# A sparse-attention and MoE kernel whose threshold pick among nine numbers on VectorE is replaced by eight pads that GpSimd writes behind the masked scores

## The chip, the cores and the metric

The kernel runs on one core of one Trainium2 chip. The metric is the device time of one execution in microseconds (us). Before the change it was 1723.53 us, the median of three runs (1721.57 to 1724.83). A core has five engines that work side by side, each in the order of its own instruction list: TensorE (PE in the profile, its weight loads are PEld), VectorE (DVE), ScalarE (ACT), GpSimd (POOL) and SyncE (SP), which here issues the transfers. An instruction that needs another engine's result waits for a semaphore, and everything behind it on its own engine waits with it.

## The reference

An attention in which every query keeps only its 32 largest scores, followed by a two-layer network with a squared ReLU:

```
scores = scale * q @ k.T                      # 8 batches, 8 heads, 576 x 576, 64 wide
kth    = the 32nd largest score of each row
scores = where(scores >= kth, scores, -1e9)
attn   = exp(scores - max) / (sum + 1e-9)
x      = attn @ v                             # heads side by side: 4608 tokens x 512
h      = x @ w_in                             # 512 x 2048
g      = s * relu(h)**2 + b
out    = g @ w_out                            # 2048 x 512
```

q, k and v are float32, the two weight matrices come in float64. Products are made of high and low halves of float32 numbers, so that they keep float32's precision.

## The kernel before, in words

**Tiles.** The scores of 128 queries against 576 keys are one tile; 288 tiles make up the attention (9 for each pair of heads, 4 pairs in a batch, 8 batches). A loop over steps (L813) keeps several tiles under way: in step i the scores of tile i + 2 are multiplied, the candidates of tile i are searched, tile i - 1 gets its cut, and tile i - 2 its threshold, its mask and its transposes. The hidden chunks of the network run between them, about one a step once a batch of attention is done, paced by `pace` (L804).

**The threshold of a tile.** VectorE takes the 8 largest of each of 8 groups of 72 scores (`groups`, L270), and from these 64 candidates, in three rounds (`chain`, L277 to L286), the 24th largest. GpSimd (`cut_at`) takes the upper 16 bits of that candidate less a half as the cut (L293), makes the bias of the exponential (L294), and clears the lower 16 bits of the candidate in place (L295). ScalarE (`side`, L301) writes `wt`: 1 for a score below the cut and -1 for the others, and adds these up into `cnt`. With n scores at or above the cut, `cnt` is 576 - 2n. GpSimd (`window`, L306) multiplies `wt` by the scores, so that those at or above the cut become negative. VectorE (`wmax`, L313) takes the 8 largest of `wt`: these are the places n + 1 to n + 8 of the row. `pick` (L318) then compares `cnt` with nine constants in `sel` and so picks the 32nd place among nine numbers, the cut candidate itself and these eight. `mask` (L323) sets the exponentials `e` to zero where the score is below that threshold `th`, and sums the rest. TensorE transposes the result (`put`, L352), ScalarE takes its high halves `ph` (L357), VectorE the low halves `pl` (L363), and TensorE multiplies with v (`attend`, L391, L392).

**What sets the order.** No scheduler moves these parts. Every step emits its parts by one of three written lists, ORDER_FIRST while weights are converted, ORDER_MAIN in most steps, ORDER_LAST from shortly before the last batch, and each engine keeps the order in which its parts were emitted. `wt`, `e`, the score bank `s_ps` and the transpose bank `tp` have one buffer each: the next transposes wait until `pl` has read the bank. At the end a row whose threshold could not be proven sets a flag, and then a second, plain and much longer path computes the whole problem again.

Of the kernel before, what the change touches and what calls it, by code (L numbers as in the profile page):

```python
# [18 lines left out]
P = 128  # L19
# [3 lines left out]
CHUNKS = [(0, 0), (1, P), (2, 2 * P + D), (3, 3 * P + D)]  # columns of each 128 queries; the last 64 sit between  # L23
# [16 lines left out]
# weight steps before the first tile  # L40
WPRE = 2
# hidden chunks before the end of a block at which the next is split, after the attention
SPL = 4
# weight pieces under way in a step
WPS = 2
ENGINES = {getattr(mybir.EngineType, e) for e in ("PE", "Activation", "DVE", "Pool", "SP")}
# the order in which a step emits the parts of the tiles under way: while the weights are
# converted, in most steps, and from shortly before the last batch
ORDER_FIRST = """
    g fetch gs sc wmax cut store av c0 sq o prep exp add sums wb xs prepo hi scale side pick  # L50
# [3 lines left out]
    g sc exp wb cut add gs wmax av prep scale prepo c0 pick wa c1 xs h gA split mask hi lows wc  # L54
# [3 lines left out]
    wb gs add sc exp wmax wa av g cut hi c0 prep wc pick c1 relu prepo h o scale split c2 mask  # L58
# [7 lines left out]
def fast_path(ctx, tc, q, k, v, w_in, w_out, s_in, b_in, out, flag):  # L66
# [48 lines left out]
    # the weights come in float64, as its bits; a step makes float32 parts of 256 columns  # L115
# [20 lines left out]
    def weight_step(n):  # L136
# [14 lines left out]
        # a float64 exponent (a zero's too) that float32 has not is farther than 221 here  # L151
# [53 lines left out]
    def prep(j, x, hl, c0, c1, rest):  # L205
        """PE transposes of k's or q's rows; returns the emitter of what reads them."""
# [65 lines left out]
    def chain(t, k):  # L272
        """Three rounds of 8 maxima; the first two leave out the lower candidates of the groups."""
        low = t.cand.rearrange("p (g n) -> p g n", n=8)[:, :, : (3, 3, 5, 5, 8)[k]]
        if k == 0:
            t.wl = sb.tile([P, 24], F32, name="wl", tag="wl", bufs=3)
# [11 lines left out]
    def cut_at(t):  # L288
        """The 24th candidate's upper 16 bits less a half, and the maximum for exp."""
# [5 lines left out]
        nc.gpsimd.memset(cut16[:, 30:31], 0)  # L295

    def side(t):
        """1 for the scores below the cut, -1 for the others, and their sum."""
        t.wt = sb.tile([P, S], F32, name="wt", tag="wt", bufs=BUFS["wt"])
        t.cnt = sb.tile([P, 2], F32, name="cnt", tag="cnt", bufs=3)  # L300
        nc.scalar.activation(  # L301
            t.wt, t.sc.bitcast(I16)[:, 1::2], AF.Sign, bias=t.half, scale=-1.0, accum_out=t.cnt[:, 0:1]
        )

    def window(t):
        nc.gpsimd.tensor_tensor(out=t.wt, in0=t.sc, in1=t.wt, op=ALU.mult)  # L306
# [808 lines left out]
```

## Time and profile before

| What | Value |
|---|---|
| Time, median of three runs | 1723.53 us |
| Lowest and highest run | 1721.57 and 1724.83 us |
| Span of the profiled execution, first to last instruction | 1721.7 us |
| PE busy | 1563.8 us, 91% |
| DVE busy | 1460.6 us, 85% |
| ACT busy | 1321.5 us, 77% |
| POOL busy | 1247.8 us, 72% |

The profile gives the span of the profiled execution and no separate figure for what lies around it; the span is 1.8 us below the median of the three runs. Shares of busy time are means over stages of unlike kind: in the first 215 us the weights are converted beside the first attention tiles, until about 301 us there is hardly any network to compute, then attention and network run together until 1376 us, and the end is mostly network. A line in the profile is named by the kernel's line, its engine, its operation, and the buffers written and read (out<-in, buffer numbers left out).

### The profile page before, as it was taken

The page shows a single profiled execution, that of the slowest core. Times are in us where ns is not written, and L with a number is a line of the kernel's source. Part 1 is how long each engine was busy: PE and PEld are TensorE (multiplying, and loading weights), DVE is VectorE, ACT ScalarE, POOL GpSimd, SP SyncE. Part 2 cuts the span into 40 slices and gives each one's busy share as a digit, 9 for nine tenths or more (in the row PEclk, how much of TensorE's full clock was granted, in tenths as well). Part 3 has the DMA queues.
Part 4 walks back from the last instruction along what each step waited for, and adds up shares of the span by engine and source line. Part 5 has one row for each costly group of instructions (what it writes and reads, how often), then busy time and mean ns, then how long its engine had stood idle before and what let it go on. Part 6 is the DMA issues. An engine that isn't in the chain of part 4 may idle for free.

```text
span 1721.7 us, 36778 instructions
## 1 busy us (share of the span) xinstructions
PE 1563.8 (91%) x10001; PEld 1352.9 (79%) x10001; DVE 1460.6 (85%) x6631; ACT 1321.5 (77%) x3042; POOL 1247.8 (72%) x2240
## 2 busy tenths in 40 slices
PE   4778878998999999999999999999999999999997
PEld 3445546877888887878798888898888879898886
DVE  6999977999999999999999989998998987786500
ACT  5777766888888888888888888888887887776532
POOL 6777746777877877777777777877777777767543
PEclk9778887999999999999999999999999999999999
DMA  4433311121221212121212121211222243332110
GB/s 126 115 103 116 94 48 49 39 66 45 53 61 37 67 41 67 39 67 45 70 41 58 45 66 37 76 40 50 57 58 64 59 111 97 92 95 78 47 28 15
DMA packets 113208, 110.25 MB, mean 64 GB/s; under 512 B 47456, under 2 KB 83296, under 8 KB 112992
## 3 DMA queue, kind: packets, MB, share of 16 engines
q1 hardware_dynamic: 112992, 107.81, 23.4%
q8 instruction: 82, 1.34, 0.3%
q14 instruction: 134, 1.10, 0.2%
HBM read 65.01 MB, written 23.86 MB: 52 GB/s over the span
## 4 chain that ended last, share of the span: by engine, by line
PE 49%; DVE 31%; ACT 7%; POOL 6%; issue 5%; DMA 1%; SPq 1%; ACTq 0%; POOLq 0%; DVEq 0%
PE h L493 16%; PE ops L517 14%; DVE e L323 6%; DVE cand L270 5%; PE s_ps L255 5%; PE tp L352 5%; DVE wl L313 3%; DVE pl L363 3%; DVE jk L318 2%; POOL wt L306 2%; PE av L391 2%; PE av L392 2%; DVE rt L142 2%; ACT wt L301 2%; PE s_ps L201 1%
## 5 line engine op out<-in xcount | busy, mean ns | idle before, releaser
L306 POOL TENSOR_TENSOR wt<-sc,wt 128x576 f32<-128x576 f32 x288 | 426.8, 1482 | 215.5 <-ACT wt L301 212.3
L493 PE MATMUL h<-x,wih 128*128 128x256 f32 x2176 | 433.6, 294 | 7.5 <-POOL x L485 4.3
L270 DVE MAX8 cand<-sc 128x8 f32<-128x72 f32 x2304 | 400.9, 218 | 4.0 <-ACT sc L264 4.0
L493 PEld LDWEIGHTS h<-x,wih 128*128 128x128 f32 x2176 | 341.4, 190 | 25.6 <-POOL x L485 16.9
L493 PE MATMUL h<-x,wil 128*128 128x256 f32 x1088 | 307.7, 283 | 0.0
L310 ACT ACTIVATE e<-sc,nb 128x576 f32<-128x576 f32 x288 | 223.0, 774 | 91.7 <-PE tq L353 69.4
L323 DVE SCALAR_TENSOR_TENSOR e<-sc,tall,e 128x576 f32<-128x576 f32 x288 | 279.8, 972 | 10.5 <-ACT e L310 9.5
L313 DVE MAX8 wl<-wt 128x8 f32<-128x576 f32 x288 | 215.5, 748 | 51.4 <-POOL wt L306 50.9
L301 ACT ACTIVATE wt<-sc,nb 128x576 f32<-128x576 int16 x288 | 223.3, 775 | 18.5 <-POOL nb L293 16.4
L352 PE MATMUL tp<-idr,e 128*128 128x128 f32 x1152 | 187.0, 287 | 54.3 <-DVE pl L363 37.8
L508 POOL TENSOR_TENSOR gl<-rt,gh 128x256 fp32r<-128x256 f32 x288 | 213.1, 740 | 28.8 <-PE ops L517 4.6
L264 ACT ACTIVATE sc<-s_ps 128x576 f32<-128x576 f32 x288 | 185.4, 644 | 63.3 <-DVE e L323 32.3
L517 PE MATMUL ops<-woh,gl 128*128 128x512 f32 x576 | 229.2, 398 | 0.9 <-POOL gl L508 0.5
L517 PE MATMUL ops<-woh,gh 128*128 128x512 f32 x576 | 227.4, 395 | 1.0 <-POOL gh L507 1.0
L517 PE MATMUL ops<-wol,gh 128*128 128x512 f32 x576 | 227.9, 396 | 0.0
L352 PEld LDWEIGHTS tp<-idr,e 128*128 128x128 f32 x1152 | 143.0, 147 | 100.6 <-DVE pl L363 54.5
L363 DVE TENSOR_TENSOR pl<-tp,ph 128x512 fp32r<-128x512 f32 x252 | 172.8, 686 | 51.9 <-ACT ph L357 50.4
L493 PEld LDWEIGHTS h<-x,wil 128*128 128x128 f32 x1088 | 207.5, 191 | 0.0
L507 POOL TENSOR_SCALAR gh<-rt 128x256 fp32r<-128x256 f32 x288 | 129.9, 451 | 94.6 <-ACT rt L502 81.4
L499 ACT ACTIVATE rt<-h 128x256 f32<-128x256 f32 x288 | 109.1, 379 | 102.1 <-PE h L493 100.6
L357 ACT ACTIVATE ph<-tp 128x512 fp32r<-128x512 f32 (+1 forms) x288 | 169.2, 587 | 16.9 <-PE av L391 12.5
L255 PE MATMUL s_ps<-ka,qs 128*128 128x288 f32 x512 | 158.0, 323 | 19.5 <-ACT qm L221 9.2
(107 smaller groups left out, 3692.3 us busy)
## 6 DMA issues: line engine op xcount, KB each, us to landing
kb<-ka SPq DMA_DIRECT2D x128, 144.0 KB, 2.5
out_dram<-osb SPq DMA_DIRECT2D x72, 128.0 KB, 2.4
raw<-in_k_dram SPq DMA_DIRECT2D x64, 128.0 KB, 2.3
x<-in_moe_w_in_dram SPq DMA_DIRECT2D x32, 256.0 KB, 3.1
x<-in_moe_w_out_dram SPq DMA_DIRECT2D x32, 256.0 KB, 2.9
xd<-avu SPq DMA_DIRECT2D x28, 288.0 KB, 2.2
raw<-in_q_dram SPq DMA_DIRECT2D x56, 128.0 KB, 2.2
raw<-in_v_dram SPq DMA_DIRECT2D x56, 128.0 KB, 2.2
```

Source lines behind the costliest of these rows:

```text
L255: nc.tensor.matmul(flat[:, hf * 288 : (hf + 1) * 288], st, kx[:, hf * 288 : (hf + 1) * 288], start=(m == 0), stop=(m == last),)
L270: nc.vector.max(t.cand[:, g * 8 : g * 8 + 8], t.sc[:, g * GW : (g + 1) * GW])
L301: nc.scalar.activation(t.wt, t.sc.bitcast(I16)[:, 1::2], AF.Sign, bias=t.half, scale=-1.0, accum_out=t.cnt[:, 0:1])
L306: nc.gpsimd.tensor_tensor(out=t.wt, in0=t.sc, in1=t.wt, op=ALU.mult)
L310: nc.scalar.activation(t.e, t.sc, AF.Exp, bias=t.nb, scale=scale)
L313: nc.vector.max(t.wl[:, 16:24], t.wt)
L323: nc.vector.scalar_tensor_tensor(t.e, t.sc, t.th, t.e, op0=ALU.is_ge, op1=ALU.mult, accum_out=t.pair.ssum[:, t.i : t.i + 1])
L352: nc.tensor.transpose(tp[:, c, :], t.e[:, c * P : (c + 1) * P], idf)
L363: nc.vector.tensor_tensor(out=pl[:, :, dst], in0=tp, in1=ph[:, :, dst].bitcast(F32), op=ALU.subtract)
L493: nc.tensor.matmul(h, wi[a][:, cc, fs], k.x[cc][:, c, :], start=(n == 0), stop=(n == last))
L508: nc.gpsimd.tensor_tensor(out=gl, in0=rt, in1=gh.bitcast(F32), op=ALU.subtract)
L517: nc.tensor.matmul(k.ops[t], g[:, ts_], wo[w][:, fc, :], start=(fc == 0 and i == 0), stop=(fc == NFC - 1 and i == 2),)
```

## The change

`pick` and its constants go. Instead GpSimd writes eight more numbers, `pads`, behind the 576 of `wt`, and the maximum over 584 columns finds the threshold as its eighth value. Pad j is (2j - 527 + cnt) * -1e30. With n scores at or above the cut, n - 24 of the eight pads are large and positive and the others large and negative, so the eighth largest of the 584 is the 32nd place of the row when n is between 24 and 31. The clearing of the candidate's lower bits (L295) goes too. The maxima, the threshold and the row's sum now stand in one buffer `chk`, nine numbers for each tile, in place of `ssum`, `tall` and the last third of `wl`.

```diff
-    sel = const.tile([P, NG + 1], F32, name="sel")
-    for j in range(NG + 1):
-        nc.gpsimd.memset(sel[:, j : j + 1], float(S - 2 * (TOPK - j)))
+    pads = const.tile([P, PADS], F32, name="pads")
+    for j in range(PADS):
+        nc.gpsimd.memset(pads[:, j : j + 1], float(2 * j - (S - 2 * 24 - 1)))
...
-            t.wl = sb.tile([P, 24], F32, name="wl", tag="wl", bufs=3)
+            t.wl = sb.tile([P, 16], F32, name="wl", tag="wl", bufs=3)
...
-        nc.gpsimd.memset(cut16[:, 30:31], 0)
...
-        t.wt = sb.tile([P, S], F32, name="wt", tag="wt", bufs=BUFS["wt"])
+        t.wt = sb.tile([P, S + PADS], F32, name="wt", tag="wt", bufs=BUFS["wt"])
...
-        nc.gpsimd.tensor_tensor(out=t.wt, in0=t.sc, in1=t.wt, op=ALU.mult)
+        nc.gpsimd.tensor_tensor(out=t.wt[:, :S], in0=t.sc, in1=t.wt[:, :S], op=ALU.mult)
+        nc.gpsimd.tensor_scalar(t.wt[:, S:], pads, t.cnt[:, 0:1], -PADK, op0=ALU.add, op1=ALU.mult)
...
-        nc.vector.max(t.wl[:, 16:24], t.wt)
-
-    def pick(t):
-        jk = sb.tile([P, NG + 1], F32, name="jk", tag="jk", bufs=1)
-        t.th = t.pair.tall[:, t.i : t.i + 1]
+        nc.vector.max(t.pair.chk[:, t.i, 0:8], t.wt)
+
+    def mask(t):
+        chk = t.pair.chk[:, t.i]
         nc.vector.scalar_tensor_tensor(
-            jk, sel, t.cnt[:, 0:1], t.wl[:, 15:24], op0=ALU.is_equal, op1=ALU.mult, accum_out=t.th
+            t.e, t.sc, chk[:, 7:8], t.e, op0=ALU.is_ge, op1=ALU.mult, accum_out=chk[:, 8:9]
         )
 
-    def mask(t):
-        nc.vector.scalar_tensor_tensor(
-            t.e, t.sc, t.th, t.e, op0=ALU.is_ge, op1=ALU.mult, accum_out=t.pair.ssum[:, t.i : t.i + 1]
-        )
...
-        nc.vector.tensor_reduce(tmin[:, 0, pr.i : pr.i + 1], pr.tall[:, :n], axis=AX.X, op=ALU.min)
+        nc.vector.tensor_reduce(tmin[:, 0, pr.i : pr.i + 1], pr.chk[:, :n, 7:9], axis=AX.XY, op=ALU.min)
...
-        nc.vector.tensor_scalar(pr.ri[:, :n], pr.ssum[:, :n], 1e-9, None, op0=ALU.add)
+        nc.vector.tensor_scalar(pr.ri[:, :n], pr.chk[:, :n, 8], 1e-9, None, op0=ALU.add)
...
-            elif op == "pick":
-                bk and pick(bk)
```

In the three lists of the order the word `pick` goes, and nothing else in them changes. VectorE's list of a step of ORDER_MAIN before, from the last round of the candidates of one tile (`wl<-cand`) over the maximum of `wt` and the pick of the tile two before it to its mask and low halves:

```order
L286 MAX wl<-cand 128x8
L270 MAX cand<-sc 128x8 x5
L313 MAX wl<-wt 128x8
L277 MAX wl<-cand 128x8
L318 SCALAR_TENSOR_TENSOR jk,tall<-sel,cnt,wl 128x9
L279 MATCH_REPLACE cand<-wl,cand 128x8x3
L270 MAX cand<-sc 128x8
L323 SCALAR_TENSOR_TENSOR e,ssum<-sc,tall,e 128x576
L363 TENSOR_TENSOR pl<-tp,ph 128x4x128
```

The same stretch of VectorE's list in the changed kernel:

```order
L289 MAX wl<-cand 128x8
L273 MAX cand<-sc 128x8 x5
L318 MAX chk<-wt 128x8
L280 MAX wl<-cand 128x8
L282 MATCH_REPLACE cand<-wl,cand 128x8x3
L273 MAX cand<-sc 128x8
L322 SCALAR_TENSOR_TENSOR e,chk<-sc,chk,e 128x576
L362 TENSOR_TENSOR pl<-tp,ph 128x4x128
```

The pick has gone from between the two first rounds of the candidates, and nothing stands in another place. GpSimd's list of such a step before, from one product `wt` over the network's halves (`gh`, `gl`) and the cut (`nb`) to the next `wt`:

```order
L306 TENSOR_TENSOR wt<-sc,wt 128x576
L507 TENSOR_SCALAR gh<-rt 128x256
L508 TENSOR_TENSOR gl<-rt,gh 128x256
L293 TENSOR_SCALAR nb<-wl 128x1
L294 TENSOR_SCALAR nb<-wl 128x1
L295 MEMSET wl 128x1
L187 TENSOR_TENSOR hl<-raw,hl 128x5x64
L306 TENSOR_TENSOR wt<-sc,wt 128x576
```

And in the changed kernel:

```order
L309 TENSOR_TENSOR wt<-sc,wt 128x576
L310 TENSOR_SCALAR wt<-pads,cnt 128x8
L507 TENSOR_SCALAR gh<-rt 128x256
L508 TENSOR_TENSOR gl<-rt,gh 128x256
L296 TENSOR_SCALAR nb<-wl 128x1
L297 TENSOR_SCALAR nb<-wl 128x1
L190 TENSOR_TENSOR hl<-raw,hl 128x5x64
L309 TENSOR_TENSOR wt<-sc,wt 128x576
L310 TENSOR_SCALAR wt<-pads,cnt 128x8
```

The pads stand right behind the product, ahead of the network's halves, and the clearing has gone from behind the two cuts. The lists of TensorE, ScalarE and SyncE are as they were.

## Rows read from the trace of the kernel before

**Rows 1.** The page's first part: the span, and the busy time of each engine with its share of the span and its instructions.

```profile
span 1721.7 us, 36778 instructions
PE 1563.8 (91%) x10001; PEld 1352.9 (79%) x10001; DVE 1460.6 (85%) x6631; ACT 1321.5 (77%) x3042; POOL 1247.8 (72%) x2240
```

**Rows 2.** Busy time by stage: start and end of the stretch, its length, then for each engine its busy us and (x) its instructions, the granted TensorE clock as a share of full speed, the DMA engines' share, and GB/s.

```profile
43.00:215.00 172.00, 134.45 (x548) 89.78 (x549) 168.92 (x699) 129.01 (x292) 127.56 (x225) 0.79 0.37 107
215.00:301.00 86.00, 65.81 (x314) 48.18 (x313) 66.05 (x330) 57.62 (x126) 46.68 (x86) 0.78 0.18 48
301.00:430.00 129.00, 116.19 (x787) 103.36 (x786) 123.10 (x563) 106.53 (x246) 96.34 (x172) 0.99 0.19 50
430.00:860.00 430.00, 401.35 (x2723) 354.41 (x2724) 405.92 (x1896) 363.12 (x838) 335.73 (x591) 1.00 0.21 55
860.00:1376.00 516.00, 497.54 (x3414) 447.90 (x3412) 477.13 (x2190) 431.17 (x999) 399.60 (x718) 1.00 0.21 54
1376.00:1677.00 301.00, 293.07 (x1940) 263.81 (x1939) 187.58 (x835) 199.96 (x468) 202.23 (x370) 0.99 0.28 79
```

**Rows 3.** What TensorE's matmuls waited for longest in the stretches from 301 to 430, 430 to 860 and 860 to 1376 us, one row for each: us in total, times, the longest.

```profile
PE tp L352 <- DVE pl L363: 7.9, 6, 2.3
...
PE tp L352 <- DVE pl L363: 17.6, 21, 1.1
...
PE tp L352 <- DVE pl L363: 9.0, 11, 1.1
```

**Rows 4.** The costliest groups of instructions by line, shapes kept apart: busy us, mean ns of one | idle us of the engine just before them, and what ended it.

```profile
L270 DVE MAX8 cand<-sc 128x8 f32<-128x72 f32 x2304 | 400.9, 218 | 4.0 <-ACT sc L264 4.0
L323 DVE SCALAR_TENSOR_TENSOR e<-sc,tall,e 128x576 f32<-128x576 f32 x288 | 279.8, 972 | 10.5 <-ACT e L310 9.5 <-ACT ka L213 0.2
L313 DVE MAX8 wl<-wt 128x8 f32<-128x576 f32 x288 | 215.5, 748 | 51.4 <-POOL wt L306 50.9
L318 DVE SCALAR_TENSOR_TENSOR jk<-sel,cnt,wl 128x9 f32<-128x9 f32 x288 | 106.2, 369 | 7.0 <-ACT e L310 0.7 <-DVE wl L277 0.7 <-ACT sc L264 0.4
...
L507 POOL TENSOR_SCALAR gh<-rt 128x256 fp32r<-128x256 f32 x288 | 129.9, 451 | 94.6 <-ACT rt L502 81.4 <-PE tp L352 10.3 <-PE ops L517 0.2
L294 POOL TENSOR_SCALAR nb<-wl 128x1 f32<-128x1 f32 x288 | 59.7, 207 | 0.0
L295 POOL MEMSET wl<- 128x1 int16 x288 | 29.3, 102 | 0.0
L426 POOL TENSOR_SCALAR avl<-ri 128x128 f32<-128x128 f32 x16 | 6.3, 411 | 0.3
```

**Rows 5.** The pick's own line: minimum, median and maximum of its duration in ns, first and last start.

```profile
L318 DVE SCALAR_TENSOR_TENSOR jk<-sel,cnt,wl x288: 211/231/1289, 30.5 to 1620.1; 128x9 f32<-128x9 f32 x144
```

**Rows 6.** The timeline of VectorE through one step (start us, us, instruction, and in brackets the idle time before it and what ended it).

```profile
912.08 0.75 DVE L313 MAX8 wl<-wt 128x8 f32<-128x576 f32 x1
912.74 0.17 DVE L277 MAX8 wl<-cand 128x8 f32<-128x24 f32 x1
912.93 0.23 DVE L318 SCALAR_TENSOR_TENSOR jk<-sel,cnt,wl 128x9 f32<-128x9 f32 x1
913.09 0.08 DVE L318 DVE_READ_ACCUMULATOR jk<-sel,cnt,wl 128x1 f32 x1
913.09 0.09 DVE L279 MATCH_VALUE_LOAD cand<-wl,cand 128x8 f32 x1
913.16 0.17 DVE L279 MATCH_REPLACE8 cand<-wl,cand 128x24 f32<-128x24 f32 x1
913.25 0.22 DVE L270 MAX8 cand<-sc 128x8 f32<-128x72 f32 x1
913.39 1.40 DVE L323 SCALAR_TENSOR_TENSOR e<-sc,tall,e 128x576 f32<-128x576 f32 x1
```

**Rows 7.** The timeline of GpSimd beside it (the two cuts and the low halves of k's or q's rows), and then of VectorE and GpSimd five us later, around another pick.

```profile
912.93 0.20 POOL L293 TENSOR_SCALAR nb<-wl 128x1 f32<-128x1 int16 x1
913.08 0.20 POOL L294 TENSOR_SCALAR nb<-wl 128x1 f32<-128x1 f32 x1
913.30 0.88 POOL L187 TENSOR_TENSOR hl<-raw,hl 128x320 fp32r<-128x320 f32 x1
...
917.92 1.25 DVE L318 SCALAR_TENSOR_TENSOR jk<-sel,cnt,wl 128x9 f32<-128x9 f32 x1
919.11 0.08 DVE L279 MATCH_VALUE_LOAD cand<-wl,cand 128x8 f32 x1
...
917.74 1.41 POOL L421 TENSOR_TENSOR avu<-avu,avl 128x576 f32<-128x576 f32 x1
```

**Rows 8.** The first and the last of 131 tiles (1 until 215 us, 10 until 301, 11 until 430, 34 until 860, 48 until 1376, 27 after) whose maximum on VectorE starts less than 0.2 us behind the end of their `wt` on GpSimd: the product and the maximum, in the timeline.

```profile
85.45 1.93 POOL L306 TENSOR_TENSOR wt<-sc,wt 128x576 f32<-128x576 f32 x1 [2.27 <-ACT wt L301]
87.42 0.76 DVE L313 MAX8 wl<-wt 128x8 f32<-128x576 f32 x1 [0.61 <-POOL wt L306]
...
1617.75 1.42 POOL L306 TENSOR_TENSOR wt<-sc,wt 128x576 f32<-128x576 f32 x1
1619.20 0.76 DVE L313 MAX8 wl<-wt 128x8 f32<-128x576 f32 x1 [1.93 <-POOL wt L306]
```

**Rows 9.** The pick's line by stage: start and end of the stretch, its length, VectorE's busy us in it with (x) the instructions, two for each pick, the granted clock, the DMA share and GB/s.

```profile
43.00:215.00 172.00, 8.38 (x53) 0.79 0.37 107
215.00:301.00 86.00, 5.94 (x32) 0.78 0.18 48
301.00:430.00 129.00, 10.54 (x50) 0.99 0.19 50
430.00:860.00 430.00, 30.92 (x168) 1.00 0.21 55
860.00:1376.00 516.00, 38.78 (x196) 1.00 0.21 54
1376.00:1677.00 301.00, 13.17 (x74) 0.99 0.28 79
```

**Rows 10.** What VectorE waited for longest over the whole span, after the output's wait at the end: us in total, times, the longest.

```profile
DVE wl L313 <- POOL wt L306: 50.9, 69, 5.4
DVE pl L363 <- ACT ph L357: 50.4, 63, 3.8
```

More of the change, by code (lines that the diff above doesn't have):

```diff
@@ L28 @@
 PW = 384
+PADS = 8
+PADK = 1.0e30
 NEG = -3.0e38
@@ L49 @@
 ORDER_FIRST = """
-    g fetch gs sc wmax cut store av c0 sq o prep exp add sums wb xs prepo hi scale side pick
+    g fetch gs sc wmax cut store av c0 sq o prep exp add sums wb xs prepo hi scale side
     split wc qk c1 lo gA c2 win relu h mask resth gC lows c3 second avout restl gB c4 put wa load
@@ L53 @@
 ORDER_MAIN = """
-    g sc exp wb cut add gs wmax av prep scale prepo c0 pick wa c1 xs h gA split mask hi lows wc
+    g sc exp wb cut add gs wmax av prep scale prepo c0  wa c1 xs h gA split mask hi lows wc
     qk resth lo side load o store relu second fetch restl c2 win gB c3 gC c4 avout sq put sums
@@ L57 @@
 ORDER_LAST = """
-    wb gs add sc exp wmax wa av g cut hi c0 prep wc pick c1 relu prepo h o scale split c2 mask
+    wb gs add sc exp wmax wa av g cut hi c0 prep wc  c1 relu prepo h o scale split c2 mask
     resth lo restl c3 qk lows xs sums gA side load win avout gC put sq gB fetch c4 second store
@@ L294, in cut_at @@
         nc.gpsimd.tensor_scalar(t.nb, t.wl[:, 0:1], -scale, 0.0, op0=ALU.mult, op1=ALU.add)
-        nc.gpsimd.memset(cut16[:, 30:31], 0)
     def side(t):
-        t.wt = sb.tile([P, S], F32, name="wt", tag="wt", bufs=BUFS["wt"])
+        t.wt = sb.tile([P, S + PADS], F32, name="wt", tag="wt", bufs=BUFS["wt"])
         t.cnt = sb.tile([P, 2], F32, name="cnt", tag="cnt", bufs=3)
         nc.scalar.activation(
-            t.wt, t.sc.bitcast(I16)[:, 1::2], AF.Sign, bias=t.half, scale=-1.0, accum_out=t.cnt[:, 0:1]
+            t.wt[:, :S], t.sc.bitcast(I16)[:, 1::2], AF.Sign, bias=t.half, scale=-1.0, accum_out=t.cnt[:, 0:1]
         )
     def window(t):
-        nc.gpsimd.tensor_tensor(out=t.wt, in0=t.sc, in1=t.wt, op=ALU.mult)
+        nc.gpsimd.tensor_tensor(out=t.wt[:, :S], in0=t.sc, in1=t.wt[:, :S], op=ALU.mult)
+        nc.gpsimd.tensor_scalar(t.wt[:, S:], pads, t.cnt[:, 0:1], -PADK, op0=ALU.add, op1=ALU.mult)
     def expo(t):
@@ L634, in fast_path @@
         pr.qs, pr.ks, pr.vs, pr.avs, pr.hl, pr.raw = [None] * 2, [None] * 2, [None] * 2, None, {}, {}
-        pr.ssum = pr.tall = None
+        pr.chk = None
         pr.cols = sorted(order)
@@ L819, in fast_path @@
         bk = tiles[i - 2] if 2 <= i <= NT + 1 else None
-        if cur is not None and cur.pair.ssum is None:
+        if cur is not None and cur.pair.chk is None:
             pr = cur.pair
-            pr.ssum = sb.tile([P, NC9], F32, name="ssum", tag="ssum", bufs=2)
-            pr.tall = sb.tile([P, NC9], F32, name="tall", tag="tall", bufs=2)
+            pr.chk = sb.tile([P, NC9, 9], F32, name="chk", tag="chk", bufs=2)
             pr.nb = sb.tile([P, 2, NC9], F32, name="nb", tag="nb", bufs=2)
```

## The prediction

> **What bounds the kernel now.** I read the busy shares first, then the busy times by stage, then what TensorE waits for, and last the lines of VectorE. Over the whole span TensorE is busy for 91% and VectorE for 85% [rows 1], which by itself makes TensorE the bound. By stage it looks different [rows 2]. From 43 to 215 us VectorE is busy for 168.92 of 172 us, 98%, and TensorE for 78%: there VectorE is the bound. From 301 to 430 us VectorE has 95% and TensorE 90%; from 430 to 860 us 94% and 93%; from 860 to 1376 us 92% and 96%; from 1376 us on TensorE has 97% and VectorE 62%. So both engines are nearly full through the middle, and what VectorE gives back is worth something only where TensorE stands idle for it: 12.8, 28.7 and 18.5 us of idle TensorE in the three middle stages (length less busy time), of which 7.9, 17.6 and 9.0 us are waits of the transposes `tp` until VectorE has made the low halves `pl` of the tile before [rows 3]. That is the place at which the change can pay after 301 us; ahead of 215 us all that VectorE saves should count.
>
> **What goes.** 288 picks of 369 ns on average, 106.2 us of VectorE's busy time [rows 4]. That is not what they cost the engine. In a plain step the pick starts at 912.93 and the next instruction at 913.09 [rows 6]: 0.16 us of the queue, since the 231 ns of its median [rows 5] reach into the next instruction. The mean is 138 ns above the median, 39.7 us over 288 tiles, and the longest pick takes 1289 ns. One of these shows why: it begins at 917.92 and ends at 919.17, while GpSimd works from 917.74 to 919.15 on a sum with two inputs [rows 7]. The pick has two tensor inputs in SBUF as well, and it ends with the other engine's instruction. I call this a hold.
>
> The Trainium skill (GPSIMD Engine Reference, section Specifications) says that GpSimd's SBUF interfaces are shared with VectorE, with contention for VectorE instructions that have two SBUF inputs. The trace agrees here (1289 ns against 231). Taken strictly the rule speaks against the change: the hold belongs to the meeting of the two engines and not to the pick, and the mask, which also has two SBUF inputs, would meet the same GpSimd instruction. That is the first rival below.
>
> How much of the hold goes: without the pick the mask would be reached 0.30 us after the place where the pick stood (913.09 to 913.39, [rows 6]), so up to 0.3 us of a hold is covered by work with one input and the rest goes over to the mask. The long one would give back 0.3 of 1.0 us, a hold under 0.3 us all of it. Bounds 0 and 0.14 us for each tile; most holds must be short, since half of the picks have none and the mean is 0.14, so I take 0.09. With the 0.16 that makes 0.25 us for each tile.
>
> **What comes.** The maximum reads 584 columns instead of 576: from 218 ns at 72 to 748 ns at 576 columns [rows 4] it is 1.05 ns a column, so 8 ns. VectorE keeps 0.24 us for each tile.
>
> GpSimd's pads, 128x8 with one tensor input: nearest rows are 207 ns for one column and 411 ns for 128 columns; from 207 at 1 to 451 at 256 columns it is 0.96 ns a column [rows 4], which makes 0.21 us. No row has a number per partition as the operand of GpSimd's instruction, so the bounds are 0.15 us (from one cut to the next, 912.93 to 913.08, [rows 7]) and 0.41 us; I take 0.2. The clearing that goes (102 ns, [rows 4]) stands elsewhere, ahead of a stretch in which GpSimd mostly waits for ScalarE, and I cost it at nothing: between 0 and 0.1 us a tile gained. GpSimd is busy for 72%, so its total is no matter. What matters is the place: the pads stand between `wt` and the maximum that waits for it. Behind the waiting maximum stand the first rounds of the candidates, the mask, and `pl`, for which the transposes wait. In 131 tiles the maximum starts less than 0.2 us behind the end of `wt`: 1 until 215 us, 10, 11, 34, 48 in the stages after that, and 27 at the end [rows 8]; the view of waits counts 69 and 50.9 us [rows 10]. There 0.2 us are added. Behind `wt` the network's halves `gh` and `gl` come 0.2 us later as well; they have slack in a step, and I cost that at nothing, up to 0.05 us a tile.
>
> The wait of the pick for `cnt` goes with it; it hid nothing (idle of 7.0 us in all, [rows 4]). The constants at the start are eight stores for nine: nothing. ScalarE, SyncE and TensorE issue the same lists.
>
> **The sum,** with half of the instruction counts in [rows 9] as tiles:
> - 43 to 215 us: 26 tiles x 0.24 = 6.2 us, VectorE is the bound and the pads lie in slack. Gain 6.
> - 215 to 301 us: 16 x 0.24 = 3.8, less 10 x 0.2 = 2.0 for pads. VectorE is idle for a quarter there. Gain 1.
> - 301 to 430 us: 25 x 0.24 = 6.0, less 11 x 0.2 = 2.2, is 3.8; the transposes wait for 7.9. Gain 3.
> - 430 to 860 us: 84 x 0.24 = 20.2, less 34 x 0.2 = 6.8, is 13.4; the transposes wait for 17.6, so it could all count. But what is late next is `ph` of ScalarE, for which `pl` waits 50.4 us over the span [rows 10], and an earlier VectorE only waits longer there. I take 60%: gain 8.
> - 860 to 1376 us: 98 x 0.24 = 23.5, less 48 x 0.2 = 9.6, is 13.9; the transposes wait for only 9.0, and TensorE is at 96%. I take half of the 9.0: gain 4.5.
> - From 1376 us on TensorE is 97% busy and VectorE waits for others; the pads lie in its idle time: 0.
>
> Together 22.5 us off the span of 1721.7, so 1699.2; the median of the runs was 1.8 us above the span, which makes 1701 us.
>
> **Rivals.**
>
> (1) The holds go over to the mask entire. VectorE then saves 0.15 us a tile: 3.9 us until 215 us, nothing until 301, 25 x 0.15 - 2.2 = 1.6 until 430, 84 x 0.15 - 6.8 = 5.8 until 860, of which 60% is 3.5, and 98 x 0.15 - 9.6 = 5.1 until 1376, of which a third is 1.7. Gain 10, time 1714. For it: the long hold in [rows 7], and a mask of 1.40 us beside the low halves `hl` [rows 6, 7]. Against it: an earlier mask can also come ahead of such an instruction, and then gains.
>
> (2) TensorE's waits for `pl` vanish altogether: 7.9 + 17.6 + 9.0 with 6 and 1.5 from the start, 42 us, time 1681. For it: the order is fixed, so a lead that VectorE wins in one step is kept until something else takes it, and earlier masks may miss GpSimd's long products. Against it: `ph` as above, and the other two thirds of a tile's path, which do not change.
>
> (3) Slower. The pads take 0.41 us rather than 0.2, with the holds passed on. A tile whose maximum waits for `wt` then loses 0.41 - 0.15 = 0.26 us: 82 such tiles from 430 to 1376 us lose 21, of which 60% reaches TensorE, 13; 21 tiles from 215 to 430 us lose 5; the start gains 4; the end loses about 1 of its 27 x 0.26. Time 1738. It decides from the point at which pads and semaphore take longer than the 0.24 us that the pick gives back. For it: half the maxima in the busy middle start at once behind `wt` [rows 8], and nothing in the trace shows this form on GpSimd. Against it: all its short instructions with one input lie between 0.10 and 0.21 us.
>
> (4) No change: what VectorE wins is spent waiting for `ph` and for the pads. 1721 to 1727 us. For it: TensorE at 96% in the longest stage. Against it: the stage at 98% of VectorE, which is certain to gain something.
>
> That the change doesn't do what it says: a row with 32 scores at or above the cut gets a threshold that nothing reaches, its sum is 0, and the plain path runs as well, many times the time. Worked out from the reference's inputs the count lies between 24 and 30 in all 36,864 rows, so I give it less than 1 in 100.
>
> **How the numbers follow.** Forecast 0.40, (1) 0.20, (2) 0.19, (3) 0.12, (4) 0.09. A change within 0.2% (3.4 us) is about what a measurement of this kernel can tell from none. Faster by more than that: the first three and little less, 0.78; within it 0.10; slower 0.12. The range goes from 1678, just under (2), to 1727, the upper end of (4); (3) and a gain above 45 us are left out.
>
> **What would show it.** Right: no line of the pick; the maximum at 756 ns; pads near 0.21 us, and VectorE's waits for them more than 50.9 us, most of the added time from 215 us on; the mean of the mask not above 972 + 50 ns [rows 4] (at 1110, 138 more, the first rival holds); TensorE's waits for `pl` in 430 to 860 us down from 17.6 to about 10; stage 43 to 215 us shorter by 6 us at the same work. Wrong: pads over 0.3 us, waits for `pl` as long as before, or a stage in the middle that becomes shorter by more than its waits for `pl`.

## The result, and the profile after

The changed kernel takes 1736.36 us (median of 4 runs, 1735.99 to 1737.29) against 1723.45 us before (median of 4, 1721.57 to 1724.83). The ratio is 1.0079, 95% interval 1.0065 to 1.0093: 12.9 us slower. The profiled execution took 1735.99 us, 1.8 us above its span.

The page's first part and its chain of waits (answers to [rows 1]; the chain gives the share of the span by engine, and the last line is that of the kernel before):

```profile
span 1734.2 us, 35701 instructions
PE 1567.4 (90%) x10001; PEld 1356.7 (78%) x10001; DVE 1399.3 (81%) x6055; ACT 1323.9 (76%) x3042; POOL 1375.0 (79%) x2239
...
PE 31%; DVE 24%; POOL 21%; ACT 12%; issue 8%; DMA 2%; SPq 1%; POOLq 0%; ACTq 0%; DVEq 0%
...
PE 49%; DVE 31%; ACT 7%; POOL 6%; issue 5%; DMA 1%; SPq 1%; ACTq 0%; POOLq 0%; DVEq 0%
```

VectorE has 61.3 us less to do and GpSimd 127.2 us more. In the chain of the kernel before, GpSimd had 6% and TensorE 49%; now GpSimd has 21% and TensorE 31%. An engine that was nearly absent from the path to the end now carries a fifth of it.

Busy time by stage, with the columns of [rows 2]:

```profile
43.00:215.00 172.00, 135.72 (x551) 90.54 (x552) 169.57 (x647) 129.83 (x293) 145.94 (x226) 0.80 0.36 107
...
430.00:860.00 430.00, 400.48 (x2709) 353.03 (x2708) 382.61 (x1714) 362.22 (x834) 369.01 (x589) 1.00 0.21 55
860.00:1376.00 516.00, 490.08 (x3348) 439.88 (x3347) 447.72 (x1966) 424.12 (x980) 441.08 (x705) 1.00 0.20 53
```

From 43 to 215 us VectorE runs 52 instructions fewer and is as busy as before (169.57 against 168.92). From 430 to 860 us it is freed by 23 us, and TensorE's idle time does not move (29.5 us against 28.7). From 860 to 1376 us TensorE's idle time grows from 18.5 to 25.9 us, while GpSimd goes from 399.60 to 441.08 of 516 us. By the timeline of the maxima, tile 156 (counted from 0) is reached at 878.3 us in both kernels, and the last tile at 1619.2 before and 1630.9 after: nothing is won or lost on balance until 878 us, and the loss falls behind it.

Three of the long waits of VectorE and ScalarE over the span (us, times, the longest), and last the second of them in the kernel before:

```profile
DVE chk L318 <- POOL wt L310: 127.1, 169, 4.0
...
ACT wt L303 <- POOL nb L296: 65.3, 83, 2.0
...
DVE pl L362 <- ACT ph L356: 51.8, 63, 4.1
...
ACT wt L301 <- POOL nb L293: 16.4, 28, 1.2
```

The maximum's wait went from 50.9 us in 69 places [rows 10] to 127.1 in 169. The second line is the one that I had no term for: ScalarE's signs, which need GpSimd's `nb`, waited 16.4 us before and wait 65.3 now.

TensorE's waits, first from 430 to 860 us, then (matmuls, and the weight load under `PEld`) from 860 to 1376 us:

```profile
PE tp L351 <- DVE pl L362: 4.8, 9, 0.8
...
PE s_ps L204 <- ACT sc L267: 10.5, 17, 1.0
...
PE tp L351 <- DVE pl L362: 0.8, 2, 0.5
...
PEld s_ps L204 <- POOL wt L310: 15.1, 18, 1.2
```

The waits for `pl` that were to go [rows 3] did go, 17.6 to 4.8 and 9.0 to 0.8 us. Others took their place: TensorE's transposes into `s_ps` (q's and k's halves, L204) now wait until ScalarE has copied the scores out of it (10.5 us, 1.1 before), and their weight loads for GpSimd (15.1 us, 4.1 before). The profile names the pads in that last line; the loads read `idr` and `hl` and not the pads, so what released them is not shown.

The groups by line that answer to [rows 4] (busy us, mean ns | idle before), then GpSimd's product after and before, and the `nb` of the kernel before:

```profile
L322 DVE SCALAR_TENSOR_TENSOR e<-sc,chk,e 128x576 f32<-128x576 f32 x288 | 273.1, 948 | 7.5 <-ACT e L314 5.7
L318 DVE MAX8 chk<-wt 128x8 f32<-128x584 f32 x288 | 219.9, 764 | 127.3 <-POOL wt L310 127.1
...
L296 POOL TENSOR_SCALAR nb<-wl 128x1 f32<-128x1 int16 x288 | 114.7, 398 | 6.3 <-DVE wl L289 3.1
...
L310 POOL TENSOR_SCALAR wt<-pads,cnt 128x8 f32<-128x8 f32 x288 | 91.9, 319 | 24.1
...
L309 POOL TENSOR_TENSOR wt<-sc,wt 128x576 f32<-128x576 f32 x288 | 427.4, 1484 | 148.8 <-ACT wt L303 145.8
...
L306 POOL TENSOR_TENSOR wt<-sc,wt 128x576 f32<-128x576 f32 x288 | 426.8, 1482 | 215.5 <-ACT wt L301 212.3
...
L293 POOL TENSOR_SCALAR nb<-wl 128x1 f32<-128x1 int16 x288 | 58.4, 203 | 18.5 <-DVE wl L286 18.4
```

The pads cost 319 ns on average. `nb`, an instruction on one number per row that nobody edited, went from 203 to 398 ns. GpSimd's and then VectorE's timeline through one step show why:

```profile
911.40 1.43 POOL L309 TENSOR_TENSOR wt<-sc,wt 128x576 f32<-128x576 f32 x1 [1.31 <-ACT wt L303]
912.92 0.27 POOL L310 TENSOR_SCALAR wt<-pads,cnt 128x8 f32<-128x8 f32 x1
913.26 0.41 POOL L507 TENSOR_SCALAR gh<-rt 128x256 fp32r<-128x256 f32 x1
913.75 0.74 POOL L508 TENSOR_TENSOR gl<-rt,gh 128x256 fp32r<-128x256 f32 x1
914.46 0.80 POOL L296 TENSOR_SCALAR nb<-wl 128x1 f32<-128x1 int16 x1
```

```profile
913.22 0.77 DVE L318 MAX8 chk<-wt 128x8 f32<-128x584 f32 x1
913.91 0.17 DVE L280 MAX8 wl<-cand 128x8 f32<-128x24 f32 x1
914.11 0.09 DVE L282 MATCH_VALUE_LOAD cand<-wl,cand 128x8 f32 x1
...
914.41 0.80 DVE L322 SCALAR_TENSOR_TENSOR e<-sc,chk,e 128x576 f32<-128x576 f32 x1
```

The product ends at 912.83, the pads begin at 912.92 and end at 913.19, the maximum begins at 913.22: the pads put 0.36 us between product and maximum, not 0.2. Behind them on GpSimd's queue stand `gh`, `gl` and only then `nb`, which starts at 914.46, just behind the mask's start at 914.41. It stands until the mask ends at 915.21, 0.80 us for a 0.2 us instruction.

The hold of [rows 7] thus works in both directions. The Trainium skill (SBUF — State Buffer, section "Who interferes with whom") says that the ports which VectorE and GpSimd share are an exclusive lock, that a VectorE instruction with two SBUF inputs contends with a GpSimd instruction that reads SBUF, and that the order of issue decides which of the two blocks. This trace agrees (`nb`, issued 0.05 us behind the mask, took 0.80 us against a median of 192 ns).

### The profile page after: what moved, and what is told of

It is laid out like the page before. It is cut to its first block, busy times and chain, and to the rows that moved or that the text cites. A ratio compares the mean times of both kernels' runs of the same rounds, so it can differ in the third digit from the quotient of the medians.

```text
span 1734.2 us, 35701 instructions
## 1 busy us (share of the span) xinstructions
PE 1567.4 (90%) x10001; PEld 1356.7 (78%) x10001; DVE 1399.3 (81%) x6055; ACT 1323.9 (76%) x3042; POOL 1375.0 (79%) x2239
## 4 chain that ended last, share of the span: by engine, by line
PE 31%; DVE 24%; POOL 21%; ACT 12%; issue 8%; DMA 2%; SPq 1%; POOLq 0%; ACTq 0%; DVEq 0%
PE h L493 10%; PE ops L517 9%; POOL wt L309 7%; DVE cand L273 4%; ACT wt L303 4%; DVE e L322 4%; DVE chk L318 3%; PE s_ps L258 3%; PE tp L351 2%; POOL gl L508 2%; POOL nb L296 2%; DVE rt L145 2%; POOL gh L507 2%; POOL x L485 2%; ACT ph L356 2%
## 5 line engine op out<-in xcount | busy, mean ns | idle before, releaser
L318 DVE MAX8 chk<-wt 128x8 f32<-128x584 f32 x288 | 219.9, 764 | 127.3 <-POOL wt L310 127.1
L322 DVE SCALAR_TENSOR_TENSOR e<-sc,chk,e 128x576 f32<-128x576 f32 x288 | 273.1, 948 | 7.5 <-ACT e L314 5.7
L303 ACT ACTIVATE wt<-sc,nb 128x576 f32<-128x576 int16 x288 | 223.2, 775 | 67.9 <-POOL nb L296 65.3
L351 PE MATMUL tp<-idr,e 128*128 128x128 f32 x1152 | 186.2, 287 | 24.8 <-DVE pl L362 12.3
L351 PEld LDWEIGHTS tp<-idr,e 128*128 128x128 f32 x1152 | 144.2, 147 | 65.3 <-DVE pl L362 22.2
L507 POOL TENSOR_SCALAR gh<-rt 128x256 fp32r<-128x256 f32 x288 | 117.2, 407 | 90.8 <-ACT rt L502 71.3
```

The source lines that it names most:

```text
L303: nc.scalar.activation(t.wt[:, :S], t.sc.bitcast(I16)[:, 1::2], AF.Sign, bias=t.half, scale=-1.0, accum_out=t.cnt[:, 0:1])
L318: nc.vector.max(t.pair.chk[:, t.i, 0:8], t.wt)
L322: nc.vector.scalar_tensor_tensor(t.e, t.sc, chk[:, 7:8], t.e, op0=ALU.is_ge, op1=ALU.mult, accum_out=chk[:, 8:9])
L351: nc.tensor.transpose(tp[:, c, :], t.e[:, c * P : (c + 1) * P], idf)
```

## The experiments

The first runs were to part two theories, which the expectations call L and H. L: the pads make the round from `nb` (GpSimd) to the signs (ScalarE) to the product (GpSimd) to the maximum (VectorE) longer, and later ones are late by that. H: the price is `nb`'s standstill beside the mask. Ratios are against the kernel before on the same chip, with 95% intervals; where runs of different chips are set against each other, I use these ratios.

**Each half alone.** Only the pads, which nobody reads; the pick stays:

```diff
+        nc.gpsimd.tensor_scalar(t.wt[:, S:], pads, t.cnt[:, 0:1], -PADK, op0=ALU.add, op1=ALU.mult)
...
-        nc.vector.max(t.wl[:, 16:24], t.wt)
+        nc.vector.max(t.wl[:, 16:24], t.wt[:, :S])
```

> The kernel before with the pads added behind wt on GpSimd, written and never read; pick, clearing and the maximum over 576 columns stay. Theory L (latency: the changed kernel is slower because the pads, 0.27 us and 0.08 us of gap, stand between wt and the maximum): nothing of VectorE is given back here, so at least as slow as the changed kernel, 1736 to 1750 us, and VectorE's waits for GpSimd at the maximum at 110 us or more. Theory H (hold: without the pick the mask starts just ahead of GpSimd's first cut nb, which then stands still for 0.6 us, 102 times of 288): the pick still delays the mask, so nb keeps its 200 ns, few holds, and the time is only a little above before, 1724 to 1732 us. Rival C (neither: the waits come and go without cost): 1723 us.

1759.48 us, 1.0208 (1.0193 to 1.0223): worse than the change itself, though the maximum hardly waits longer than before (56.6 us against 50.9, where L wanted 110). `nb` is at 202 ns, so H has no part in it. The pick's line shows 118 ns more than its mean of 369, 34 us of VectorE's time over 288 tiles: the pads shift `gl` to beside the pick. In one step `gl` runs from 932.98 to 933.72 us, and the pick stands from 933.21 to 933.76.

```profile
L324 DVE SCALAR_TENSOR_TENSOR jk<-sel,cnt,wl 128x9 f32<-128x9 f32 x288 | 140.1, 487 | 7.0 <-DVE wl L282 1.5 <-ACT rt L505 0.4
```

The pick goes and no pads come: the changed kernel, less its pads. The clearing is gone here too:

```diff
-        nc.gpsimd.tensor_scalar(t.wt[:, S:], pads, t.cnt[:, 0:1], -PADK, op0=ALU.add, op1=ALU.mult)
...
-        nc.vector.max(t.pair.chk[:, t.i, 0:8], t.wt)
+        nc.vector.max(t.pair.chk[:, t.i, 0:8], t.wt[:, :S])
```

> The changed kernel without the pads: the maximum reads 576 columns and its eighth number is taken as the threshold, which is exact only for rows with 24 scores at the cut, so that the choice of the threshold is left out for the others. Theory L: the pads were the price, so 1695 to 1712 us. Theory H: mask and nb still meet (mask 1.19 us behind the end of wt, nb 1.20 us behind it), nb stays near 400 ns on average, and the time is 1718 to 1735 us.

1709.54 us, 0.9927 (0.9913 to 0.9941). The pick, with the clearing, is worth 12.9 us (1722.41 less 1709.54), and the pads take 1.52% back (0.9927 to 1.0079), about 26 us. No run takes out the clearing alone. By its profiled execution (1706.72 us) tile 29's maximum starts at 216.5 us, tile 156's at 861.8 and the last at 1602.8, against 218.9, 878.3 and 1619.2 before: 2.4 us are won until 219 us, 14.1 more until 878 and nothing after that. Against the changed kernel's 218.4, 878.3 and 1630.9 the pads lose 1.9, 14.6 and 11.6 us in the same three parts: the zero until 878 us was a gain and a loss of one size. The mask's line shows that a part of the holds was handed on, 972 to 1036 ns:

```profile
L321 DVE SCALAR_TENSOR_TENSOR e<-sc,chk,e 128x576 f32<-128x576 f32 x288 | 298.3, 1036 | 20.5 <-ACT e L313 20.1
```

**What of the pads costs.** The changed kernel, pads written but not read:

```diff
-        nc.vector.max(t.pair.chk[:, t.i, 0:8], t.wt)
+        nc.vector.max(t.pair.chk[:, t.i, 0:8], t.wt[:, :S])
```

> The changed kernel with the pads written as in it, but the maximum reads the 576 columns ahead of them, so it waits for wt alone; the threshold is exact only for rows with 24 scores at the cut. Theory P (path: what the pads cost is the 0.40 us that the maximum waits for them): near the kernel without pads, 1708 to 1716 us. Theory S (shift: the pads move the rest of GpSimd's list by 0.35 us, so that its instructions meet VectorE's instructions with two inputs, and one of the two stands still): 1725 to 1745 us, with the durations of nb, hl or the mask above those without pads.

1727.65 us, 1.0034 (1.0022 to 1.0046), as theory S had it. Most of the price stays when nobody waits for the pads: 1.07% of 1.52% (from 0.9927 to 1.0034, of 0.9927 to 1.0079). ScalarE's waits for `nb` are as long as in the changed kernel:

```profile
DVE chk L318 <- POOL wt L309: 78.5, 108, 3.4
...
ACT wt L303 <- POOL nb L296: 64.3, 85, 1.9
```

If the place ahead of `gh`, `gl` and `nb` is what costs, the same unread pads behind `nb` must be cheap. A first form of this wrote them into `wt`:

```diff
+    def spare(t):
+        nc.gpsimd.tensor_scalar(t.wt[:, S:], pads, t.cnt[:, 0:1], -PADK, op0=ALU.add, op1=ALU.mult)
...
             elif op == "cut":
                 prv and cut_at(prv)
+                bk and spare(bk)
```

> The changed kernel with the pads written behind the two nb instead of behind wt, for the tile before, and never read; the maximum takes 576 columns, so the threshold is inexact. GpSimd does as much as with the pads unread behind wt (1727.7 us). Theory S (their place ahead of gh, gl and nb is the price): nb's mean back near 200 ns and 1708 to 1716 us. Rival O (GpSimd's longer list is the price wherever they stand): 1722 to 1732 us.

1740.31 us, 1.0095 (1.008 to 1.0109), above both ranges, and no test: there is one buffer of `wt`, so the next tile's signs wait for the pads (`ACT wt L306 <- POOL wt L300`, 90.1 us). With a buffer of their own:

```diff
...
+        sp = sb.tile([P, PADS], F32, name="sp", tag="sp", bufs=1)
+        nc.gpsimd.tensor_scalar(sp, pads, t.cnt[:, 0:1], -PADK, op0=ALU.add, op1=ALU.mult)
```

> The pads written behind the two nb into a buffer of their own, never read; the maximum takes 576 columns, so the threshold is inexact. The same GpSimd work as with the pads unread behind wt (1727.7 us), but gh, gl and nb keep their place behind wt, and ScalarE waits for nothing new. Theory S (place ahead of gh, gl and nb): 1709 to 1717 us, ScalarE's waits for nb near 16 us as before. Rival O (mere time on GpSimd): 1722 to 1732 us.

1714.81 us, 0.9949 (0.9935 to 0.9962), in theory S's range, although the same instruction is held more (451 ns):

```profile
L301 POOL TENSOR_SCALAR sp<-pads,cnt 128x8 f32<-128x8 f32 x288 | 129.8, 451 | 27.4
...
ACT wt L307 <- POOL nb L296: 27.3, 31, 1.4
```

So of the pads' 1.52%, the instruction itself takes 0.22% (0.9927 to 0.9949, 3.8 us), its place ahead of `gh`, `gl` and `nb` 0.85% (to 1.0034, 14.6 us), and the maximum's wait for it 0.45% (to 1.0079, 7.8 us). The part of the place holds the delay and the standstills that come with it: `nb` takes 393 ns on average with the unread pads ahead of it and 197 with them behind, the mask 1044 and 963. The two runs differ in the pads' buffer too; with the pads ahead, no wait of the signs for them is listed. TensorE's transposes into `s_ps` wait for the copied scores 9.0 us over the span without pads, 8.2 with them behind `nb`, 22.6 with them ahead and unread, and 22.1 in the changed kernel. The intervals are about 0.13% wide to each side, so the last two are told apart from nothing with ease, the first narrowly.

**Is it the standstill of `nb`?** Two runs move `nb` out of the mask's way. First the cuts are emitted ahead of `gh` and `gl`:

```diff
-    g sc exp wb cut add gs wmax av prep scale prepo c0  wa c1 xs h gA split mask hi lows wc
+    cut g sc exp wb add gs wmax av prep scale prepo c0  wa c1 xs h gA split mask hi lows wc
...
-    wb gs add sc exp wmax wa av g cut hi c0 prep wc  c1 relu prepo h o scale split c2 mask
+    wb gs add sc exp wmax wa av cut g hi c0 prep wc  c1 relu prepo h o scale split c2 mask
```

> The changed kernel with the cut (two nb) emitted ahead of the network's halves gh and gl on GpSimd instead of behind them, in the two later lists. nb then ends about 1 us ahead of the mask. Theory H: nb near 200 ns, and the loss goes: 1705 to 1722 us. Theory L: the pads still stand ahead of the maximum, 1730 to 1737 us.

1741.04 us, 1.0118 (1.0099 to 1.0136). `nb` is back at 202 ns, and nothing is won. Over the span the signs' wait for `nb` fell from 65.3 to 0.8 us and TensorE's for the copied scores from 22.1 to 3.3, but its transposes' wait for `pl` rose from 12.3 to 34.5. What meets the mask now is `gl`, and the mask pays: in one step `gl` ends at 919.26 us, and the mask, begun at 918.89, takes 0.99 us, where 0.80 is its least. The mask's line, three waits of this run, and the last two of them in the changed kernel:

```profile
L322 DVE SCALAR_TENSOR_TENSOR e<-sc,chk,e 128x576 f32<-128x576 f32 x288 | 318.5, 1106 | 9.7 <-ACT e L314 9.4
...
ACT wt L303 <- POOL nb L296: 0.8, 2, 0.5
...
PE s_ps L204 <- ACT sc L267: 3.3, 8, 0.8
...
PE tp L351 <- DVE pl L362: 34.5, 40, 1.9
...
PE s_ps L204 <- ACT sc L267: 22.1, 37, 1.1
...
PE tp L351 <- DVE pl L362: 12.3, 18, 1.7
```

Second, a maximum over 256 columns in the pick's old place, into a buffer that nobody reads, delays the mask until `nb` is through; the same in the kernel without pads gives its price:

```diff
                 cur and chain(cur, int(op[1]))
+                op == "c0" and bk and plain(bk)
...
+    def plain(t):
+        jk = sb.tile([P, 8], F32, name="jk", tag="jk", bufs=1)
+        nc.vector.max(jk, t.sc[:, 0:256])
```

> The changed kernel with a maximum over 256 columns (one input, about 0.35 us) on VectorE in the place that the pick had, so that the mask starts some 0.2 us later, behind nb. Theory H (nb's standstill beside the mask is a large part of the price): nb's mean falls from 398 to under 280 ns, and the time is 1722 to 1734 us, lower than the changed kernel although VectorE has more to do. Rival P (what counts is the pads' wait and place): nb falls or not, and the time rises to 1738 to 1755 us.

> The same long instruction in the kernel without pick and pads (threshold inexact as there): its price by itself. If VectorE's place is worth its time: 1718 to 1735 us, against 1709.5 without it. If it is hidden: 1708 to 1713 us.

1749.97 us, 1.0150 (1.0135 to 1.0164), with pads, and 1718.36 us, 0.9969 (0.996 to 0.9978), without: 31.6 us (1.81%) for the pads, not less than 1.52%, though `nb` stands at 200 ns. With the pads the signs still wait for it longer, 39.0 us against 15.9 without. The mask took part of the holds again, 1020 ns against 948 in the changed kernel; without pads, behind the same long instruction, it takes 985:

```profile
L326 DVE SCALAR_TENSOR_TENSOR e<-sc,chk,e 128x576 f32<-128x576 f32 x288 | 293.8, 1020 | 1.3 <-ACT e L314 0.6
...
L296 POOL TENSOR_SCALAR nb<-wl 128x1 f32<-128x1 int16 x288 | 57.5, 200 | 7.4 <-DVE wl L289 3.0
```

H, as the whole of the price, falls by both runs. A hold taken from one instruction turned up at another each time, and the time did not follow `nb`.

**The pads on another engine.** VectorE writes them some time ahead of the maximum:

```diff
...
             elif op == "gs":
+                bk and padv(bk)
```

with `padv` the same instruction on `nc.vector`.

> The changed kernel with the pads written by VectorE ahead of the last five groups of the step, so that the maximum waits for wt alone. VectorE has 0.1 to 0.16 us a tile more than in the kernel without pads. Theory L: 1705 to 1718 us. Theory H: nb beside the mask again, 1720 to 1735 us.

1723.26 us, 1.0000 (0.9989 to 1.001): as the kernel before. `nb` is at 202 ns, but this instruction with a single tensor input is held by GpSimd's product too, 536 ns on average (one starts at 909.20 us and ends at 910.14, the product beside it at 910.11):

```profile
L316 DVE TENSOR_SCALAR wt<-pads,cnt 128x8 f32<-128x8 f32 x288 | 154.5, 536 | 12.3 <-ACT wt L303 12.0
```

The same, directly ahead of the maximum, with GpSimd's pads gone as there:

```diff
...
+        nc.vector.tensor_scalar(t.wt[:, S:], pads, t.cnt[:, 0:1], -PADK, op0=ALU.add, op1=ALU.mult)
         nc.vector.max(t.pair.chk[:, t.i, 0:8], t.wt)
```

> The changed kernel with the pads written by VectorE directly ahead of the maximum instead of ahead of the last five groups. A hold by GpSimd's product wt then covers time in which the maximum would wait for wt anyway. Theory R (holds were the price): 1709 to 1718 us, with fewer us in the pads' line than the 154.5 us of the other placing. Rival N (any further instruction of VectorE in the step costs its time): 1720 to 1730 us.

1735.37 us, 1.0078 (1.0064 to 1.0092): above both ranges, and no gain over the change. In the timeline the maximum starts 0.31 us behind the pads' start (913.64 to 913.95), since it reads what they write; from the pick to the next, independent instruction it was 0.16 us [rows 6].

The first of these with the constants in PSUM, in columns of the bank of `tq` that are free:

```diff
+    tq, pads_ps = tqs[0:D], tqs[:, 400 : 400 + PADS]
+    nc.vector.tensor_copy(pads_ps, pads)
```

> The changed kernel with the pads written by VectorE ahead of the last five groups, from constants in PSUM instead of SBUF; the result is exact. Holds were 96 us of that line with the constants in SBUF (1723.3 us). If they go: the pads' mean falls from 536 to under 250 ns and the time is 1710 to 1718 us. If VectorE's further instruction is the price: 1719 to 1725 us.

1742.47 us, 1.0113 (1.0098 to 1.0129), above both ranges. The holds are gone (218 ns), but the pads now wait for TensorE's transposes into that bank:

```profile
L316 DVE TENSOR_SCALAR wt<-tq,cnt 128x8 f32<-128x8 f32 x288 | 62.9, 218 | 155.2 <-PE tq L356 151.1 <-ACT wt L303 3.3 <-ACT sc L267 0.5
```

ScalarE writes them, behind the product in program order, and in the other run right behind the signs:

```diff
...
+        nc.scalar.activation(t.wt[:, S:], pads, AF.Identity, bias=big, scale=t.cnt[:, 0:1])
```

> The changed kernel with the pads written by ScalarE, behind the window and the squared ReLU of a step, as (cnt * a_j + 1) * 1e30 with a_j = -1 / (527 - 2j), which has the same signs. GpSimd's list has neither pads nor clearing, VectorE's no pick. Theories P and S alike: near the kernel without pads, 1709 to 1718 us, where ScalarE's 0.2 us a tile are covered (it is busy for 77%); above 1723 us where the maximum then waits for ScalarE.

> The same with ScalarE's pads right behind the signs, ahead of the ReLU, so that they are written while GpSimd still makes the product and the maximum cannot wait for them. 1708 to 1716 us; above the other placing only if the wait for cnt on ScalarE delays the ReLU.

1727.54 us, 1.0040 (1.0027 to 1.0053), and 1733.55 us, 1.0065 (1.005 to 1.0079); the second was to stay under 1716. The instruction takes 391 ns there, nearly the same every time (377 to 408), and lengthens another queue of the same round: TensorE waits 17.2 and 20.7 us for the copied scores, 9.0 without pads.

**The pick itself.** A maximum over 24 columns in the pick's place, without pads and with them, was to tell a plain instruction's price from the holds:

```diff
...
+        nc.vector.max(jk, t.sc[:, 0:24])
...
```

> The kernel without pick and pads, with a maximum over 24 columns of the scores (one input, about 0.17 us) in the pick's place on VectorE; the choice of the threshold is left out as there. Theory Q (the pick cost its place in VectorE's queue, 0.16 us a tile): 1716 to 1722 us. Theory R (the pick cost its holds of 0.14 us a tile beside GpSimd): within 4 us of the kernel without pick and pads, 1706 to 1713 us.

> The changed kernel with one more VectorE instruction, the maximum over 24 columns that cost nothing in the pick's place there, between the first two rounds of the candidates. It delays the mask by 0.16 us, behind the start of nb. Theory H (the meeting of mask and nb is part of the price): nb's mean falls from 398 to below 300 ns and the time falls although work is added, 1724 to 1733 us. Rival (the pads' wait and GpSimd's later list are the whole price): 1736 to 1740 us.

1710.13 us, 0.9937 (0.9925 to 0.9949), and 1735.17 us, 1.0076 (1.0062 to 1.0090): no difference from the kernels without it, and neither run decides anything. The instruction falls between two that depend on each other, which start 0.20 us apart without it and 0.22 us with it:

```profile
913.93 0.18 DVE L280 MAX8 wl<-cand 128x8 f32<-128x24 f32 x1
914.03 0.17 DVE L321 MAX8 jk<-sc 128x8 f32<-128x24 f32 x1
914.15 0.09 DVE L282 MATCH_VALUE_LOAD cand<-wl,cand 128x8 f32 x1
```

The pick moved to directly ahead of the mask, in the kernel before (the other two lists alike):

```diff
-    g sc exp wb cut add gs wmax av prep scale prepo c0 pick wa c1 xs h gA split mask hi lows wc
+    g sc exp wb cut add gs wmax av prep scale prepo c0 wa c1 xs h gA split pick mask hi lows wc
```

> The kernel before with the pick emitted right ahead of the mask in all three lists, behind the second round and the group of the next tile; the instructions are the same. GpSimd's low halves gl are mostly done by then. Theory R (holds were the pick's price): the pick's mean falls from 369 to below 300 ns, and the time to 1708 to 1717 us. Rival N (the pick costs its place in the queue wherever it stands): 1719 to 1724 us.

1744.81 us, 1.0139 (1.0121 to 1.0157); the numbers of both theories were missed. The mask needs the pick's result and starts 0.32 us behind its start (912.39 to 912.71), twice the 0.16 us of its old place, and its mean duration is up from 369 to 434 ns.

Last, the kernel before with the pick's nine constants in PSUM, so that it has one tensor input in SBUF:

```diff
+    tq, sel_ps = tqs[0:D], tqs[:, 400 : 400 + NG + 1]
+    nc.vector.tensor_copy(sel_ps, sel)
...
-            jk, sel, t.cnt[:, 0:1], t.wl[:, 15:24]
+            jk, sel_ps, t.cnt[:, 0:1], t.wl[:, 15:24]
```

> The kernel before with the pick's nine constants in PSUM instead of SBUF, in columns of the bank tq that are free; nothing else is changed, and the result is exact. Theory R (the pick's price are its holds, which need two SBUF inputs): its duration is near 300 ns at all times, its maximum under 500 ns, and the time 1706 to 1715 us. Rival N (the pick's place in the queue is its price): holds gone or not, 1719 to 1726 us.

1716.5 us, 0.9953 (0.9940 to 0.9967): it beats both kernels and computes the same, though above theory R's range. No pick is held; minimum, median and maximum were 211, 231 and 1289 ns [rows 5]:

```profile
L318 DVE SCALAR_TENSOR_TENSOR jk<-tq,cnt,wl x288: 167/228/232, 30.6 to 1609.3; 128x9 f32<-128x9 f32 x144
...
L318 DVE SCALAR_TENSOR_TENSOR jk<-tq,cnt,wl 128x9 f32<-128x9 f32 x288 | 65.5, 227 | 18.5 <-PE tq L355 4.3 <-ACT sc L264 0.4 <-ACT hl L195 0.4
```

So 0.47% of the 0.73% come back with its holds. How the other 0.26% divide is open: this kernel still has the clearing and the pick's place in the queue, though a plain instruction in that place cost nothing that shows, and VectorE is idle ahead of the pick for 18.5 us against 7.0 [rows 4], of which 4.3 are waits for TensorE's transposes into that bank.

## Why the prediction was wrong

The forecast was 1701 us, in a range of 1678 to 1727, with 0.78 for faster. The kernel became slower, 9 us above the range. Point by point:

- *The maximum 8 ns longer, the pads' wait above 50.9 us, TensorE's waits for `pl` down to about 10 us.* All three signs came: 16 ns, 127.1 us, 4.8 us. They show that VectorE did become earlier against TensorE. They did not bear out the time, because TensorE then waited for `s_ps`. Beside them one sign of being wrong came, pads over 0.3 us (319 ns), and one of being right stayed out, a first stage 6 us shorter.
- *The gain of the pick.* The sum came to 22.5 us with the pads already taken off; pick and clearing gone, without pads, are worth 12.9. From 219 to 878 us 14.1 us came without pads, where the forecast had 1, 3 and 8 after 11.0 us for the pads, so the pick's own worth was set too high there as well. Two stages missed altogether. "VectorE is the bound and the pads lie in slack. Gain 6" fails: 2.4 us came, and with the pads 0.5. VectorE's weight instruction (L149, two inputs) is held longer there: 438 ns before, 456 without the pick, 534 with the pads; 64 times 78 ns is 5.0 us, more than the 1.9 us that the pads lose there. A pair of them takes 1.42 us from 40.57 on, while GpSimd works on `hl` from 40.45 to 41.37, behind its pads; before, that `hl` ran from 39.40 to 40.31 and the pair took 0.75 us. And the 4.5 us from 860 to 1376 us did not come even without pads, for TensorE's waits for `pl` only fell from 9.0 to 7.3 us there. Of the 138 ns of holds the mask took over 64 (972 to 1036), close to the 0.05 us that I had assumed. Rival (1), whose terms add up to 10.7 and not 10, had the pads taken off too and was not met either.
- *The pads 0.2 us.* The instruction alone takes 0.27 us, with 0.09 us between the product and it, and 319 ns on average with its holds. The upper bound of 0.41 was the nearer one. I had picked the value from rows in which one-input instructions follow each other.
- *"Behind `wt` the network's halves come 0.2 us later as well; they have slack in a step, and I cost that at nothing, up to 0.05 us a tile."* This is the step that turned the sign: 0.85%, 14.6 us, 0.05 us for each of 288 tiles. That is the upper bound that I had written down and then set to nothing, and `nb` behind the halves I had left out altogether. ScalarE's signs wait for it (16.4 to 65.3 us), and the copy of the scores out of `s_ps`, which stands on ScalarE's queue as well, is late for TensorE (4.7 to 22.1 us). That this chain alone carries the price is not shown: with the cuts ahead of `gh` and `gl` both waits went and the time did not fall. GpSimd's 28% of idle time counted for nothing: its largest part, 215.5 us, stood ahead of the product as a wait for those signs, at the other end of the same round.
- *Rival (3), 1738 us, chance 0.12,* had the size of the pads and of the time nearly right, 1.6 us off, but for a reason that is the smaller part: the maximum's longer wait is 7.8 us of about 26.

What stays open is how the 14.6 us divide between the later start of `gh` and `gl`, which feed TensorE, and that of `nb`; the change of order that parts them also moved a hold onto the mask.

## What to carry to other kernels

An engine that is idle for a quarter of the time is not a place with room: look at what its queue holds behind the new instruction, and whether one of those starts the round that the instruction is part of. A short instruction that is moved off a full engine should not be put between two steps of a round that goes through several engines. A hold between VectorE and GpSimd is best removed at its cause (one operand moved to PSUM brought 0.47%; for the pads it cost 1.13%, as TensorE writes that bank too), since a hold that is only shifted is paid by the next instruction.

## What the runs showed of the hardware

- A GpSimd instruction with one number per row and one input stands still beside VectorE's two-input mask: `nb` 192 ns at the median, 821 ns at most. ScalarE's short instruction never varied by more than 31 ns (377 to 408).
- A one-input scalar operation of VectorE in SBUF is held as well: 170 ns at least, 385 at the median, 1514 at most; from PSUM 177, 225 and 228. The Trainium skill (the page and section named above) counts `tensor_scalar` among the operations that can contend with GpSimd for the shared ports, and the runs agree.
- VectorE's maximum starts 0.31 us behind the pads, and the mask 0.32 us behind the pick, whose results they read; from the pick to an independent instruction it is 0.16 us. It is no rule for all dependent pairs: the value load of the candidates' second step starts 0.20 us behind the maximum that it reads. An independent instruction of 24 columns put between those two cost nothing that these runs can tell.
